# First products drained ahead of the slot's splits, and one difference of each pair a slot later

## The chip, the cores and the metric

The kernel runs on one core of one Trainium2 chip. The metric is the device time of one execution in microseconds; the time before is the median of three runs. A trace of one execution, taken by the hardware profiler, gives every instruction's start and length on the five engines: PE (TensorE, with PEld for its weight loads), DVE (VectorE), ACT (ScalarE), POOL (GpSimd) and SP (SyncE, which issues the transfers).

## The reference

```python
attn_out = _attn_ref(q, k, v, mem_k, mem_v)           # local attention, 4 x 8 x 768 x 64
x = attn_out.transpose(0, 2, 1, 3).reshape(3072, 512)
h = x @ w_in                                          # 512 -> 2048
x = (h * np.clip(h + 3.0, 0.0, 6.0) / 6.0) @ w_out    # 2048 -> 512
logits = x @ w_gate                                   # 8 experts
P = np.exp(logits - logits.max())
for _ in range(8):
    P /= P.sum(1, keepdims=True) + 1e-09
    P /= P.sum(0, keepdims=True) + 1e-09
    P *= N / E
for e in range(8):
    h = np.maximum(x @ w1[e], 0.0)                    # 512 -> 1024
    out += P[:, e:e + 1] * (h @ w2[e])                # 1024 -> 512
```

The change lies in the last loop, the eight experts.

## The kernel before, in words

All numbers are 32-bit. Every product is made of three matmuls: each operand is split into a rounded high part and the rest, and `passes` (lines 226 to 228) adds high x high, high x low and low x high in PSUM. ACT makes the high part, DVE the low part by subtracting.

The 3072 tokens are three blocks of 1024. One block with one expert is an n, so n runs from 0 to 23: block one is n = 0 to 7, block two 8 to 15, block three 16 to 23. In each n both expert products are done with seven products of half-size matrices in place of eight, so sums and differences of quarters of the operands stand around them.

- First products make h. `first_product` is a plain one: six matmuls of 512 columns into a bank ga or gc. `first_out` takes its result out of the bank (a drain): for k = 2 and p = 4 first ACT copies it (line 914), then DVE adds it into a tile g (line 920); p = 5 has only the add, p = 2 and 3 only a copy by ACT (line 916). In blocks two and three the last four of an n's first products (form `deep2`) are split further, with 256 columns; `deep_out` drains them (DVE line 903), and there several partial products follow one another in the same bank ga: the next matmul into ga needs the drain before it.
- `positive` makes a drained quarter non-negative on ACT (line 926), and POOL multiplies it by the gate's weights (line 933).
- Second products take h. `make(n, mi, part)` prepares the operand of product mi of n over four slots: part 0 splits its weights on ACT (line 843) and, where the operand is a difference of quarters of h, makes that on DVE for both halves (`g_sum`, line 959); parts 1 and 2 make the high halves on ACT (`oh`, line 979), parts 2 and 3 the low halves on DVE (`ol`, line 984). `second_out` adds a second product's result into y on DVE (line 1013).
- `w1_hi` (ACT line 806) and `w1_lo` (DVE line 811) split the weights of the first products. A low part is kept in DRAM and reloaded when the same weights come again, so that line 811 stands in block two only for weights that are new there, those of `deep2`, and in block three nowhere.

The order is written out by hand. The main loop goes through slots; a slot has one first product of n + 1 and one quarter of a second product of n on PE, and then issues, in this order on each engine: `second_out` of the slot before, `make`, the low parts of weights, a store, `positive` for the slot before, and last `first_out` of this slot's plain product and the next weights. Each engine works off its own queue in order.

Of the kernel before, what the change touches and what calls it, by code (L numbers as in the profile page):

```python
# [64 lines left out]
def attn_moe_moe(ctx: ExitStack, tc: tile.TileContext, qk, vw, wi, wo, wa, wb, wg, out):  # L65
# [4 lines left out]
    NE = wb.shape[0]  # L70
# [471 lines left out]
    def sinkhorn():  # L542
# [13 lines left out]
        for _ in range(8):  # L556
# [44 lines left out]
    SUMS = {"T1": ("B11", "B12", "B11"), "T2": ("T1", "B22", "T1"), "T3": ("B12", "B22", "B12"),  # L601
            "T4": ("T2", "B21", "T2")}
    X_ORDER = ("B21", "B11", "T1", "T2", "T3", "B22", "T4")
    NM = NSB * NE
# [224 lines left out]
    def w2_load(m):  # L829
        if m < 7 * NM:  # L830
            e, a = m // 7 % NE, SECOND[m % 7][0]
            s = w2s[m] = w2s_p.tile([128, 4, 256], F32, tag="w2s", name="w2s")
            if a >= S1:
                nc.sync.dma_start(out=s, in_=ws2[e][:, W2S[a]])
                return
            for g in range(2):
                of = wb[e, g].rearrange("p (c a d) -> p c a d", c=2, a=4)[:, :, {A11: 0, A12: 2, A22: 3}[a]]
                nc.sync.dma_start(out=s[:, 2 * g:2 * g + 2], in_=of)

    def w2_hi(m):  # L840
        if m < 7 * NM:
            hi = w2r_p.tile([128, 4, 256], F32R, tag="w2h", name="w2h", bufs=2)
            nc.scalar.activation(out=hi, in_=w2s[m], func=AF.Copy)  # L843
            w2[m] = hi
# [9 lines left out]
    def w2_lo_load(m):  # L854

        if 7 * NE <= m < 7 * NM:
            lo = w2l[m] = w2r_p.tile([128, 4, 256], F32R, tag="w2l", name="w2l", bufs=2)
            nc.sync.dma_start(out=lo.bitcast(F32), in_=wl2[m % (7 * NE)])

    def w2_lo_store(m):  # L860
        if m < 7 * NE:
            nc.sync.dma_start(out=wl2[m], in_=w2[m][1].bitcast(F32))
# [42 lines left out]
    def first_out(n, k, p):  # L905

        ps, b, i = ch[FIRST[p][2], k], FIRST_OUT[p], k // 2
        more = p == 4 and n >= NE
        for v in [b] * (p in (2, 3, 6)) + ["B21"] * more:
            if k % 2 == 0:  # L910
                gq[n, v, i] = g_p.tile([128, 2, HB], F32, tag="g", name="g", bufs=NG)
        g = gq[n, b, i][:, k % 2]
        if more:
            nc.scalar.activation(out=gq[n, "B21", i][:, k % 2], in_=ps, func=AF.Copy)  # L914
        if p in (2, 3):
            nc.scalar.activation(out=g, in_=ps, func=AF.Copy)
        elif p == 6:
            nc.scalar.activation(out=g, in_=ps, func=AF.Relu)
        else:
            nc.vector.tensor_tensor(out=g, in0=g, in1=ps, op=ALU.add)  # L920
# [33 lines left out]
    def g_sum(n, b, i):  # L954
        to, x, y = SUMS[b]
        o = gq[n, to, i]
        if n == NM - 1 and b == "T1":
            o = g_p.tile([128, 2, HB], F32, tag="g", name="g", bufs=NG)
        nc.vector.tensor_tensor(out=o, in0=gq[n, x, i], in1=gq[n, y, i], op=ALU.subtract)  # L959
        gq[n, b, i] = o  # L960

    def make(n, mi, part):

        m, b = 7 * n + mi, SECOND[mi][1]
        if part == 0:
            w2_hi(m)
            w2_lo_load(m)
            if b in SUMS and (n < NM - 1 or b in ("T2", "T4")):
                for i in range(2):
                    g_sum(n, b, i)  # L970
        if part == 1:
            w2_lo(m)
            w2_load(m + 1)
        if part == 3:
            w2_lo_store(m)
        if part in (1, 2):
            i = part - 1
            hi = op_p.tile([128, 2, HB], F32R, tag="oh", name="oh", bufs=3)
            nc.scalar.activation(out=hi, in_=gq[n, b, i], func=AF.Copy)  # L979
            op[m, i] = hi  # L980
        if part in (2, 3):
            i = part - 2
            lo = op_p.tile([128, 2, HB], F32R, tag="ol", name="ol", bufs=3)
            nc.vector.tensor_tensor(out=lo, in0=gq[n, b, i], in1=op[m, i].bitcast(F32), op=ALU.subtract)  # L984
            op[m, i] = op[m, i], lo
# [90 lines left out]
    with tc.manual_schedule():  # L1076
# [19 lines left out]
        for i, (pe, b, f) in enumerate(steps):  # L1096
# [74 lines left out]
            n = b + 1 if pe else 0  # L1171
# [49 lines left out]
        for n in range(NM):  # L1221
            for mi in range(7):
                for r in range(4):
                    i = at[n, mi - 1, r] if mi else at[n, 0, 0] - 4 + r
# [23 lines left out]
        for i, (h, o) in enumerate(order):  # L1248
            end = o and o[:2] == (NM - 1, 6)
            if h:  # L1250
                if h[1] in FORM:
                    for r in range(2):
                        deep_product(*h, r)
                        if o:
                            second_product(*o, (r,))
                else:
                    first_product(*h)
            if h and h[1] in FORM:
                pass
            elif end:  # L1260
                last_product(o[2])
            elif o:
                second_product(*o)
            if work and (i % 3 != 1 or i == 1) and next(work, 0) == 0:
                work = None
            if i in sums:
                x_sum(*sums[i])
            if before:
                second_out(*before)
            before = None if end else o  # L1270
            if end:
                last_out(o[2])
            if i in ends:
                g_sum(NM - 1, *ends[i])
            if h and h[1] in FORM:
                deep_out(*h, 0)
                while lows:
                    do, n = lows.pop(0)
                    do(n)
            for m in makes.get(i, ()):  # L1280
                make(*m)
            while lows:
                do, n = lows.pop(0)
                do(n)
            if i in gates_due:
                positive_gated(*gates_due.pop(i))
            for _ in range(2 if o and o[1] == 0 else 1):
                if left:
                    store(*left.pop(0))
            for w in after:  # L1290
                positive(*w)
            after = []
            if h and h[1] in FORM:
                n, _, p = h
                deep_out(*h, 1)
                if h[1] == DEEP2 and p > 1:
                    gates_due[i + (12 if n == NM - 1 and p == 3 else 1)] = n, p - 2
                if (h[1], p) == (DEEP, 2) and n >= 2:
                    gate_load(n)
                g = W1_AT[h]  # L1300
                if g:
                    lows.append((w1_lo, g + AHEAD - 1))
                    lows.append((w1_load, g + AHEAD + 3))
                else:
                    w1_load(AHEAD + 3)
                for m in range(AHEAD - 2 if g == 0 else 0):
                    w1_lo_store(m)
                w1_lo_store(g + AHEAD - 2)
            elif h:
                n, k, p = h  # L1310
                first_out(*h)
                if p in quarters:
                    after = [(n, k, quarters[p])]
                g = W1_AT[n, k // 2 * 2, p]
                if k % 2 == 0:
                    lows.append((w1_lo, g + AHEAD - 1))
                    w1_lo_store(g + AHEAD - 2)
            if h and (h[1] in FORM or h[1] % 2):
                if h[1] not in FORM:
                    w1_load(g + AHEAD + 3)  # L1320
                w1_lo_load(g + AHEAD)
                w1_hi(g + AHEAD)
            if i in fours:
                rows = []
                for q in range(2):
                    t = out_p.tile([128, HB], F32, tag="o", name="xs", bufs=NO)
                    nc.sync.dma_start(out=t, in_=x_source(*fours[i], q))
                    rows.append(t)
                quarter_work = i + 3, x_quarters(fours[i][1], *rows, nc.gpsimd)
            elif quarter_work and i >= quarter_work[0] and (i - quarter_work[0]) % 2 == 0:  # L1330
                if next(quarter_work[1], 0) == 0:
                    quarter_work = None
            for sb, r in halves.get(i, ()):
                x_half_load(sb, r + 2)
                if r >= 2:
                    x_half(r)
                    lows.append((x_half_low, r))
            if o and o[0] == NM - 1:
                for do, j in last.get(o[1:], ()):
                    do(j)  # L1340
            elif o and o[0] % NE == NE - 1 and o[1:] in ((5, 3), (6, 3)):
                left += [(o[0] // NE, j + 4 * (o[1] == 5)) for j in range(4)]
# [55 lines left out]
```

## Time and profile before

| | us |
|---|---|
| median of 3 runs (lowest, highest) | 2508.87 (2508.67, 2510.55) |
| profiled execution, its own time | 2509.96 |
| its span, from the first to the last instruction | 2508.2 |
| PE busy | 2491.2 |
| DVE busy | 1959.7 |
| ACT busy | 1444.9 |
| POOL busy | 910.8 |

The span is 1.8 us shorter than the execution's own time. PE's granted clock is 1.0 of full speed in every slice. The busy times overlap; what an engine does beside PE costs nothing as long as PE does not wait for it.

### The profile page before, as it was taken

The page shows a single profiled execution, that of the slowest core. Times are in us where ns is not written, and L with a number is a line of the kernel's source. Part 1 is how long each engine was busy: PE and PEld are TensorE (multiplying, and loading weights), DVE is VectorE, ACT ScalarE, POOL GpSimd, SP SyncE. Part 2 cuts the span into 40 slices and gives each one's busy share as a digit, 9 for nine tenths or more (in the row PEclk, how much of TensorE's full clock was granted, in tenths as well). Part 3 has the DMA queues.
Part 4 walks back from the last instruction along what each step waited for, and adds up shares of the span by engine and source line. Part 5 has one row for each costly group of instructions (what it writes and reads, how often), then busy time and mean ns, then how long its engine had stood idle before and what let it go on. Part 6 is the DMA issues. An engine that isn't in the chain of part 4 may idle for free. (4 is left out here: it accounts for less than half of the span.)

```text
span 2508.2 us, 37845 instructions
## 1 busy us (share of the span) xinstructions
PE 2491.2 (99%) x13525; PEld 2170.5 (87%) x13525; DVE 1959.7 (78%) x2432; ACT 1444.9 (58%) x2647; POOL 910.8 (36%) x705
## 2 busy tenths in 40 slices
PE   9999999999999999999999999999999999999999
PEld 8999999999878888888888888888888888888887
DVE  8866656576689999999986778777887677677677
ACT  8666652122365655556666655665566666555664
POOL 0155656564025544544442323232223322122320
PEclk9999999999999999999999999999999999999999
DMA  8689979877466666666777777666776677776664
GB/s 212 187 274 324 299 262 306 279 270 233 134 212 209 226 209 232 224 222 226 229 239 246 265 253 245 226 208 231 249 265 223 227 228 227 225 233 211 214 220 153
DMA packets 373753, 586.72 MB, mean 234 GB/s; under 512 B 30323, under 2 KB 227132, under 8 KB 373564
## 3 DMA queue, kind: packets, MB, share of 16 engines
q1 hardware_dynamic: 373280, 584.06, 71.5%
q8 instruction: 106, 1.74, 0.3%
q14 instruction: 83, 0.68, 0.1%
q10 hardware_dynamic: 284, 0.24, 0.0%
HBM read 443.57 MB, written 140.61 MB: 233 GB/s over the span
## 5 line engine op out<-in xcount | busy, mean ns | idle before, releaser
L933 POOL TENSOR_TENSOR g<-g,pb 128x512 f32<-128x512 f32 x304 | 533.2, 1766 | 1223.9 <-ACT g L926 818.6
L979 ACT ACTIVATE oh<-g 128x1024 fp32r<-128x1024 f32 x336 | 355.3, 1057 | 420.6 <-PE oa L228 200.5
L984 DVE TENSOR_TENSOR ol<-g,oh 128x1024 fp32r<-128x1024 f32 x336 | 470.9, 1402 | 91.7 <-ACT oh L979 91.5
L645 POOL TENSOR_TENSOR fr<-fr 128x256 f32<-128x256 f32 x320 | 270.7, 847 | 188.2 <-DMA fr<-in_wa_dram 100.5
L226 PE MATMUL ga<-xo,w1h 128*128 128x512 f32 (+1 forms) x864 | 314.8, 364 | 4.3 <-DVE g L903 3.4
L227 PE MATMUL ga<-xo,w1h 128*128 128x512 f32 (+1 forms) x864 | 312.2, 361 | 0.0
L228 PE MATMUL ga<-xo,w1l 128*128 128x512 f32 (+1 forms) x864 | 312.2, 361 | 0.0
L227 PE MATMUL oa<-ol,w2h 128*128 128x512 f32 x760 | 297.9, 392 | 1.5 <-DVE ol L984 1.4
L226 PE MATMUL oa<-oh,w2h 128*128 128x512 f32 x760 | 297.1, 391 | 0.0
L228 PE MATMUL oa<-oh,w2l 128*128 128x512 f32 x760 | 295.9, 389 | 0.0
L959 DVE TENSOR_TENSOR g<-g 128x1024 f32<-128x1024 f32 x192 | 290.6, 1553 | 0.0
L806 ACT ACTIVATE w1h<-w1s 128x512 fp32r<-128x512 f32 (+1 forms) x416 | 250.4, 602 | 47.6 <-issue 19.1
L926 ACT ACTIVATE g<-g 128x512 f32<-128x512 f32 x288 | 179.5, 623 | 124.0 <-DVE g L920 123.5
L920 DVE TENSOR_TENSOR g<-g,ga 128x512 f32<-128x512 f32 x192 | 130.5, 680 | 116.6 <-ACT g L914 113.4
L399 ACT ACTIVATE t<-ph,half 128x384 f32<-128x384 f32 x128 | 74.8, 584 | 241.4 <-PE ph L228 235.6
L226 PEld LDWEIGHTS ga<-xo,w1h 128*128 128x128 f32 x864 | 162.5, 188 | 40.3 <-DVE g L903 7.7
L843 ACT ACTIVATE w2h<-w2s 128x1024 fp32r<-128x1024 f32 x168 | 177.0, 1054 | 34.6 <-DMA w2s<-in_wb_dram 19.9
L226 PE MATMUL gc<-xo,w1h 128*128 128x512 f32 (+1 forms) x544 | 195.3, 359 | 1.0 <-ACT g L901 1.0
L228 PE MATMUL gc<-xo,w1l 128*128 128x512 f32 (+1 forms) x544 | 194.5, 357 | 0.0
L227 PE MATMUL gc<-xo,w1h 128*128 128x512 f32 (+1 forms) x544 | 194.3, 357 | 0.0
L227 PEld LDWEIGHTS ga<-xo,w1h 128*128 128x128 f32 x864 | 162.5, 188 | 28.3
L228 PEld LDWEIGHTS ga<-xo,w1l 128*128 128x128 f32 x864 | 162.4, 188 | 25.1
(184 smaller groups left out, 5774.7 us busy)
## 6 DMA issues: line engine op xcount, KB each, us to landing
w1l<-wl SPq DMA_DIRECT2D x232, 256.0 KB, 4.4
w2l<-wl SPq DMA_DIRECT2D x112, 512.0 KB, 3.7
w1s<-ws SPq DMA_DIRECT2D x192, 256.0 KB, 4.9
w2s<-ws SPq DMA_DIRECT2D x96, 512.0 KB, 5.6
ws<-fr SPq DMA_DIRECT2D x80, 512.0 KB, 5.1
w2s<-in_wb_dram SPq DMA_DIRECT2D x144, 256.0 KB, 4.3
wl<-w1l SPq DMA_DIRECT2D x128, 256.0 KB, 4.3
wl<-w2l SPq DMA_DIRECT2D x56, 512.0 KB, 4.9
```

Source lines behind the costliest of these rows:

```text
L226: nc.tensor.matmul(ps, wh, xh, start=start, stop=False, skip_group_check=more)
L227: nc.tensor.matmul(ps, wh, xl, start=False, stop=False, skip_group_check=more)
L228: nc.tensor.matmul(ps, wl, xh, start=False, stop=stop, skip_group_check=more)
L645: nc.gpsimd.tensor_tensor(out=o, in0=a, in1=b, op=f)
L806: nc.scalar.activation(out=w1_part(g, w1[g]), in_=w1_part(g, w1s[g]), func=AF.Copy)
L843: nc.scalar.activation(out=hi, in_=w2s[m], func=AF.Copy)
L920: nc.vector.tensor_tensor(out=g, in0=g, in1=ps, op=ALU.add)
L926: nc.scalar.activation(out=g, in_=g, func=AF.Relu)
L933: nc.gpsimd.tensor_tensor(out=g, in0=g, in1=p, op=ALU.mult)
L959: nc.vector.tensor_tensor(out=o, in0=gq[n, x, i], in1=gq[n, y, i], op=ALU.subtract)
L979: nc.scalar.activation(out=hi, in_=gq[n, b, i], func=AF.Copy)
L984: nc.vector.tensor_tensor(out=lo, in0=gq[n, b, i], in1=op[m, i].bitcast(F32), op=ALU.subtract)
```

## The change

For n from 8 on, `first_out` of a plain first product is issued before the slot's `make` calls and weights instead of after them. And from the second products of n = 7 on, the second of the two differences that `make` issues in part 0 (`g_sum` for half 1) goes to part 1, one slot later.

```diff
             if b in SUMS and (n < NM - 1 or b in ("T2", "T4")):
-                for i in range(2):
+                for i in range(1 if n >= NE - 1 else 2):
                     g_sum(n, b, i)
         if part == 1:
             w2_lo(m)
             w2_load(m + 1)
+            if b in SUMS and (NE - 1 <= n < NM - 1 or n == NM - 1 and b in ("T2", "T4")):
+                g_sum(n, b, 1)
...
                 while lows:
                     do, n = lows.pop(0)
                     do(n)
+            elif h and h[0] >= NE:
+                first_out(*h)
             for m in makes.get(i, ()):
                 make(*m)
             while lows:
...
                 n, k, p = h
-                first_out(*h)
+                if n < NE:
+                    first_out(*h)
                 if p in quarters:
                     after = [(n, k, quarters[p])]
```

No instruction is added or taken away. The queues of PE, POOL and SP have the same order as before; those of DVE and ACT change. Two places show it, both in the stretch in which the plain first products of n = 12 end and its `deep2` products begin, beside second products of n = 11.

DVE, before: ga is the bank of the plain products with p = 4 and then of `deep2`, gc that of p = 5; L984 is a low half ol, L959 a difference, L811 a low part of weights, L1013 an add into y.

```order
L984 TENSOR_TENSOR ol_16993<-g_16276,oh_16969 128x1024
L920 TENSOR_TENSOR g_16911<-g_16911,ga_16845 128x512
L1013 TENSOR_TENSOR y_14574<-y_14574,oa_16593 128x512
L959 TENSOR_TENSOR g_15787<-g_16045,g_15787 128x1024
L959 TENSOR_TENSOR g_15788<-g_16276,g_15788 128x1024
L811 TENSOR_TENSOR w1l_17019<-w1s_16838,w1h_16979 128x512
L920 TENSOR_TENSOR g_16911<-g_16911,ga_16866 128x512
L920 TENSOR_TENSOR g_16953<-g_16953,gc_16894 128x512
L1013 TENSOR_TENSOR y_14437<-y_14437,ob_17005 128x512
L984 TENSOR_TENSOR ol_17068<-g_15787,oh_17045 128x1024
L811 TENSOR_TENSOR w1l_17070<-w1s_16887,w1h_17028 128x512
L920 TENSOR_TENSOR g_16953<-g_16953,gc_16913 128x512
```

DVE, of the change, the same twelve instructions (lines after 972 are two higher, so that 984 is now 986 and 1013 now 1015):

```order
L920 TENSOR_TENSOR g_16907<-g_16907,ga_16844 128x512
L986 TENSOR_TENSOR ol_16996<-g_16274,oh_16970 128x1024
L1015 TENSOR_TENSOR y_14574<-y_14574,oa_16593 128x512
L920 TENSOR_TENSOR g_16907<-g_16907,ga_16866 128x512
L959 TENSOR_TENSOR g_15787<-g_16041,g_15787 128x1024
L811 TENSOR_TENSOR w1l_17020<-w1s_16837,w1h_16979 128x512
L920 TENSOR_TENSOR g_16948<-g_16948,gc_16894 128x512
L959 TENSOR_TENSOR g_15788<-g_16274,g_15788 128x1024
L1015 TENSOR_TENSOR y_14437<-y_14437,ob_17005 128x512
L920 TENSOR_TENSOR g_16948<-g_16948,gc_16913 128x512
L986 TENSOR_TENSOR ol_17069<-g_15787,oh_17046 128x1024
L811 TENSOR_TENSOR w1l_17071<-w1s_16887,w1h_17027 128x512
```

Each drain L920 has moved up by one to three places, and the second difference L959 has moved down past L811 and a drain. Behind both lists the same rows follow: the first `deep2` drain (L903 from ga), L984 or L986, the drain from gb, the add into y, the next L903 from ga.

ACT at the same place, before: L979 is a high half oh, L916 and L914 are copies out of a bank, L843 and L806 high parts of weights, L926 makes a quarter non-negative.

```order
L979 ACTIVATE oh_16969<-g_16276 128x1024
L916 ACTIVATE g_16953<-ga_16866 128x512
L806 ACTIVATE w1h_16979<-w1s_16838 128x512
L914 ACTIVATE g_16995<-ga_16845 128x512
L843 ACTIVATE w2h_17013<-w2s_16948 128x1024
L926 ACTIVATE g_16911<-g_16911 128x512
L914 ACTIVATE g_16995<-ga_16866 128x512
L806 ACTIVATE w1h_17028<-w1s_16887 128x512
L979 ACTIVATE oh_17045<-g_15787 128x1024
```

ACT, of the change:

```order
L916 ACTIVATE g_16948<-ga_16866 128x512
L981 ACTIVATE oh_16970<-g_16274 128x1024
L806 ACTIVATE w1h_16979<-w1s_16837 128x512
L914 ACTIVATE g_16993<-ga_16844 128x512
L914 ACTIVATE g_16993<-ga_16866 128x512
L843 ACTIVATE w2h_17015<-w2s_16950 128x1024
L926 ACTIVATE g_16907<-g_16907 128x512
L806 ACTIVATE w1h_17027<-w1s_16887 128x512
L981 ACTIVATE oh_17046<-g_15787 128x1024
```

The copy L914 of the second product now stands right behind that of the first, and the weights' L843 and the L926 that feeds POOL stand behind both.

## Rows read from the trace of the kernel before

**Rows 1.** The page, busy time, share of the span and instructions of each engine.

```profile
PE 2491.2 (99%) x13525; PEld 2170.5 (87%) x13525; DVE 1959.7 (78%) x2432; ACT 1444.9 (58%) x2647; POOL 910.8 (36%) x705
```

**Rows 2.** PE's waits from 1290 to 1860 us: total, times, longest.

```profile
PE ga L226 <- DVE g L903: 2.9, 7, 1.5
PE ga L226 <- ACT g L926: 0.8, 2, 0.5
```

**Rows 3.** Timeline of PE near 1610 us: start, length, instruction, idle time before.

```profile
1603.80 0.39 PE L226 MATMUL ob<-oh,w2h 128*128 128x512 f32 x1
...
1613.19 0.39 PE L228 MATMUL ob<-oh,w2l 128*128 128x512 f32 x1
1613.49 0.36 PE L226 MATMUL ga<-more,w1h 128*128 128x256 f32 x1
...
1616.75 0.39 PE L226 MATMUL ga<-xo,w1h 128*128 128x256 f32 x1 [0.21 <-DVE g L903]
```

**Rows 4.** Timeline of DVE in the same stretch.

```profile
1601.08 1.23 DVE L984 TENSOR_TENSOR ol<-g,oh 128x1024 fp32r<-128x1024 f32 x1 [1.45 <-ACT oh L979]
1602.57 0.69 DVE L920 TENSOR_TENSOR g<-g,ga 128x512 f32<-128x512 f32 x1 [0.26 <-ACT g L914]
...
1603.77 3.46 DVE L959 TENSOR_TENSOR g<-g 128x1024 f32<-128x1024 f32 x2
1607.15 0.68 DVE L811 TENSOR_TENSOR w1l<-w1s,w1h 128x512 fp32r<-128x512 f32 x1
...
1612.67 0.67 DVE L903 TENSOR_TENSOR g<-g,ga 128x512 f32<-128x512 f32 x1
1613.26 1.63 DVE L984 TENSOR_TENSOR ol<-g,oh 128x1024 fp32r<-128x1024 f32 x1
...
1616.02 0.67 DVE L903 TENSOR_TENSOR g<-g,ga 128x512 f32<-128x512 f32 x1
```

**Rows 5.** Timeline of ACT in the same stretch.

```profile
1599.98 1.06 ACT L979 ACTIVATE oh<-g 128x1024 fp32r<-128x1024 f32 x1 [3.54 <-PE oa L228]
...
1601.42 0.62 ACT L806 ACTIVATE w1h<-w1s 128x512 fp32r<-128x512 f32 x1
1601.95 0.59 ACT L914 ACTIVATE g<-ga 128x512 f32<-128x512 f32 x1
1602.42 1.06 ACT L843 ACTIVATE w2h<-w2s 128x1024 fp32r<-128x1024 f32 x1
1603.38 0.62 ACT L926 ACTIVATE g<-g 128x512 f32<-128x512 f32 x1
1604.00 0.60 ACT L914 ACTIVATE g<-ga 128x512 f32<-128x512 f32 x1
...
1610.86 1.06 ACT L979 ACTIVATE oh<-g 128x1024 fp32r<-128x1024 f32 x1 [1.77 <-PE ob L228]
```

**Rows 6.** Timeline of POOL in the same stretch.

```profile
1604.08 2.07 POOL L933 TENSOR_TENSOR g<-g,pb 128x512 f32<-128x512 f32 x1 [8.50 <-ACT g L926]
1609.17 1.29 POOL L933 TENSOR_TENSOR g<-g,pb 128x512 f32<-128x512 f32 x1 [3.03 <-ACT g L926]
1612.52 3.54 POOL L933 TENSOR_TENSOR g<-g,pb 128x512 f32<-128x512 f32 x2 [2.06 <-ACT g L926]
```

**Rows 7.** Timelines of POOL and DVE in block one, near 822 us.

```profile
820.80 2.27 POOL L933 TENSOR_TENSOR g<-g,pb 128x512 f32<-128x512 f32 x1
...
821.84 1.77 DVE L811 TENSOR_TENSOR w1l<-w1s,w1h 128x512 fp32r<-128x512 f32 x1
```

**Rows 8.** Timelines of PE and DVE at the same place of block three.

```profile
2150.11 0.28 PE L226 MATMUL ga<-more,w1h 128*128 128x256 f32 x1
...
2151.14 0.68 DVE L903 TENSOR_TENSOR g<-g,ga 128x512 f32<-128x512 f32 x1
...
2152.92 0.28 PE L226 MATMUL ga<-xo,w1h 128*128 128x256 f32 x1
```

**Rows 9.** Timeline of PE at the same place of n = 15.

```profile
1847.06 0.39 PE L226 MATMUL ga<-xo,w1h 128*128 128x256 f32 x1 [1.49 <-DVE g L903]
```

## The prediction

> **What bounds the kernel now.** I read the page first: PE is busy for 2491.2 of 2508.2 us [rows 1], so only its waits can be won, and whatever makes it wait longer is paid in full. Then PE's waits over block two: 2.9 us for DVE's drain L903 and 0.8 us put down to ACT's L926 [rows 2]. The timelines show where both lie: at one place of each n, where its `deep2` products begin. There the matmuls into ga come in three groups, and each needs the drain of the one before.
>
> From the second group (1613.49) to the third (1616.75) it takes 3.26 us [rows 3], in block three from 2150.11 to 2152.92, 2.81 [rows 8]. So a place costs 0.45 us now. DVE is what is late: behind 1602.57 no row of its shows idle time before it, its queue has been full since, and the two L903 come at 1612.67 and 1616.02 [rows 4]. There are eight places, n = 8 to 15; those of n = 9 to 14 are alike, n = 15 has a longer wait, 1.49 us [rows 9]. In block three, where L811 is gone, the second L903 ends 1.10 us before PE needs it (2151.14 + 0.68 against 2152.92) [rows 8].
>
> **The change part by part.** The same instructions run, the transfers keep their order, and the matmuls too. So the question is whether DVE reaches the two L903 sooner or later. Durations for that:
> - A 512-wide DVE instruction hands over after 0.60 (1612.67 to 1613.26), a 1024-wide one of 1.23, with the same overlap of 0.08, after 1.14 [rows 4].
> - On ACT 0.47 to 0.53 after a 512-wide one, 0.96 after a 1024-wide one (1602.42 to 1603.38) [rows 5]. L926 takes 0.62, and POOL's multiply starts 0.08 behind it (1604.00, 1604.08) [rows 5, 6].
> - A copy L914 starts 0.20 after PE's group is over (1603.80, 1604.00) [rows 3, 5].
> - DVE and POOL shut each other out. A multiply alone takes 1.29; that of 1604.08 took 2.07, so it stood until 1604.86, when the first difference (from 1603.77) had run 1.09; then the second difference stood until the multiply ended at 1606.15, and DVE's next instruction began 1.00 later, at 1607.15 [rows 4, 6]. L811 can be shut out too: 1.77 against 0.68, with its end 0.54 after the multiply's [rows 7]. A drain out of PSUM is not: L903 at 1612.67 took 0.67 under a multiply [rows 4, 6]. Who asks first, runs first.
>
> Now the queues of the change at this place. ACT: L916 has gone ahead, so behind L979 (1599.98) come L806 at 1600.94 and the first L914 at 1601.47, 0.48 sooner than now. But the drain that waits for it now heads DVE's queue, ahead of the L984 that could run at 1601.08. So DVE starts at 1602.08 in place of 1601.08: the drain, L984 at 1602.68, L1013 at 1603.82, free at 1604.42. The second L914 cannot start before 1604.00, since PE is not done sooner; it ends at 1604.60, the drain starts at 1604.62, the first difference at 1605.22 (now 1603.77, with that drain still to come: 0.85 us net late).
>
> ACT's L843 and L926 now stand behind that second L914: 1604.47 and 1605.43 to 1606.05. The first multiply asks at 1606.13; the first difference lets go at 1605.22 + 1.09 = 1606.31. By 0.18 the multiply is first. It runs to 1607.60, and L811, next on DVE, hands over at 1608.06 in place of 1606.96. Then the drain from gc, and at 1608.66 the second difference. Meanwhile ACT has done L806, L979 (1606.48) and L926 (1607.44 to 1608.06), so the second multiply runs under the drain from 1608.14 to 1609.43, and the difference hands over at 1610.43. L1013, the drain of the last plain product at 1611.03, L984 from 1611.63, letting go at 1612.72. The third multiply asks at 1612.52, as now, since the L979 ahead of it waits for PE until 1610.86 both times. It is first by 0.20, runs to 1614.01, and L811 hands over at 1614.47. So the first L903 starts at 1614.47 against 1612.67, and PE, 0.15 after its end, at 1615.29 against 1613.49. The fourth multiply follows when L811 lets go (about 1614.5 to 1615.8) and holds the next L984, which hands over at 1616.8; then the drain of gb and L1013; the second L903 at 1618.0 against 1616.02. PE goes on at 1618.73 in place of 1616.75: **2.0 us lost per place**.
>
> The six like places make 12.0. Those of n = 8 and n = 15 have the same steps and one or two more splits in DVE's queue (0.60 to 1.14 each), in which a multiply can fall; for these I take 2.5 each, 5.0. Block three: without L811 DVE has 1.1 us to spare behind the last drain [rows 8] and the 0.85 of lateness fits into it, so 0. The differences that move elsewhere (a slot later, at three other products of each n) end in L984; PE waits for none in this stretch [rows 2], and ACT's oh of the second half stands waiting for PE there (1599.98 after 3.54 us, 1610.86 after 1.77) [rows 5], so 0 again; if that cover went, a late L979 would first delay the L914 behind it on ACT, then the drains. Sum 17.0: 2509.96 + 17.0 = 2527.0 for an execution like the profiled one, whose time is 1.1 us above the median; on the median 2508.87 + 17.0 = **2525.9**.
>
> Bounds per place. Below: if the shut-outs disappear, DVE's late start is made up and PE's loss goes, a gain of 0.45. Above: one more full shut-out, 1.29 less the 0.6 it would find covered, 2.7 in all. I stand near the upper end because two of the three orders are settled by 0.18 and 0.20 us, and the handovers above repeat within 0.06.
>
> **The rivals.**
> - *The third multiply comes second.* If DVE is 0.2 us sooner at 1612.5, L811 goes first (free at 1613.3 in place of 1614.47), only the next L984 is held, and the second L903 comes 0.5 to 0.6 late. Eight places: 2513.3. For it: 0.20 is small. Against: that instant hangs on the end of the second multiply, which hangs on ACT alone.
> - *No change.* If the first multiply asks 0.18 later, L811 goes first, the second difference is held by the first multiply alone, DVE reaches the first L903 at 1612.2, and the second, held by the third multiply as now, at 1616.0. The loss stays at 0.45 a place: 2509.
> - *Faster.* The drains do not need what POOL holds, so that multiplies that fall under L920 and L903 cost DVE nothing. If all four fall so, DVE reaches the second L903 by 1615.2 instead of 1616.02, and PE's losses go: six times 0.45, and for n = 8 and 15 what the waits hold beside the six short ones of 0.21, 3.7 less 1.3 [rows 2, 3]; 5.1 in all, 2503.8. It decides when the first and the third multiply ask 0.2 us later than worked out. [...]
>
> **How the numbers follow.** The measurement can tell about 0.2%, 5.0 us: 2503.9 to 2513.9. Forecast 0.60 (2519 to 2531, its own range, 1.3 to 2.7 a place), third multiply second 0.14 (2511 to 2517, half of it beyond 2513.9), no change 0.16 (2506 to 2512), faster 0.10 (2501 to 2506, six in ten below 2503.9). That makes slower 0.60 + 0.07 = 0.67, faster 0.06, same 0.27. The range goes down from 2531 until two in ten are left out: to 2508.
>
> **What would show it.** Right: PE's waits for L903 between 1290 and 1860 grow from 2.9 us to 15 or more, none appear in block three; at each place of n = 9 to 14 L811 lasts 1.8 us; DVE idles about 2.5 us before the drain that waits for L914 (now 1.45 + 0.26). Wrong: L811 at 0.68 with PE's waits unchanged or gone; or waits at a new name, L984 before a second product, which would mean that the difference moved by a slot is what is late.

## The result and the profile after

The changed kernel takes 2529.98 us (median of 6 runs, 2527.95 to 2533.16) against 2508.77 for the kernel before in the same comparison (6 runs, 2508.49 to 2510.55): 1.0085 times as long, 95% interval 1.0072 to 1.0098, so 21.2 us slower. The forecast was 2525.9, slower, with a range of 2508 to 2531. Place, mechanism and sign came out as worked; 4.1 us are missing in the sum.

The page of the profiled execution (2533.16 us, its span 2531.4), which answers to [rows 1]:

```profile
PE 2501.7 (99%) x13525; PEld 2181.1 (86%) x13525; DVE 1946.1 (77%) x2432; ACT 1445.8 (57%) x2647; POOL 922.6 (36%) x705
```

The span has grown by 23.2 us. PE is busy 10.5 us longer with the same 13525 matmuls, and idle 12.7 us longer (29.7 against 17.0). The idle time is of the kind that was forecast, though less of it than the 17.0 of the sum. The longer busy time was not in the sum.

PE's waits from 1290 to 1880 us, against [rows 2] (total, times, longest); in block three, 1880 to 2470, PE waits for no engine:

```profile
PE ga L226 <- DVE g L903: 17.1, 11, 2.9
```

Now the place of n = 12 that the prediction worked through, against [rows 3 to 6]. It comes 13.37 us later than before (ACT's L981, the former L979, at 1613.35 against 1599.98), so 13.37 is to be taken from each start. DVE's timeline:

```profile
1615.45 0.69 DVE L920 TENSOR_TENSOR g<-g,ga 128x512 f32<-128x512 f32 x1 [2.39 <-ACT g L914]
...
1618.06 0.69 DVE L920 TENSOR_TENSOR g<-g,ga 128x512 f32<-128x512 f32 x1 [0.19 <-ACT g L914]
1618.67 1.22 DVE L959 TENSOR_TENSOR g<-g 128x1024 f32<-128x1024 f32 x1
1619.80 1.78 DVE L811 TENSOR_TENSOR w1l<-w1s,w1h 128x512 fp32r<-128x512 f32 x1
1621.51 0.68 DVE L920 TENSOR_TENSOR g<-g,gc 128x512 f32<-128x512 f32 x1
1622.11 1.90 DVE L959 TENSOR_TENSOR g<-g 128x1024 f32<-128x1024 f32 x1
...
1625.12 1.21 DVE L986 TENSOR_TENSOR ol<-g,oh 128x1024 fp32r<-128x1024 f32 x1
1626.26 1.77 DVE L811 TENSOR_TENSOR w1l<-w1s,w1h 128x512 fp32r<-128x512 f32 x1
1627.95 0.67 DVE L903 TENSOR_TENSOR g<-g,ga 128x512 f32<-128x512 f32 x1
1628.55 1.69 DVE L986 TENSOR_TENSOR ol<-g,oh 128x1024 fp32r<-128x1024 f32 x1
...
1631.36 0.68 DVE L903 TENSOR_TENSOR g<-g,ga 128x512 f32<-128x512 f32 x1
```

ACT's timeline at the same place:

```profile
1614.84 0.58 ACT L914 ACTIVATE g<-ga 128x512 f32<-128x512 f32 x1
1617.43 0.60 ACT L914 ACTIVATE g<-ga 128x512 f32<-128x512 f32 x1 [2.01 <-PE ga L228]
1617.93 1.05 ACT L843 ACTIVATE w2h<-w2s 128x1024 fp32r<-128x1024 f32 x1
1618.88 0.62 ACT L926 ACTIVATE g<-g 128x512 f32<-128x512 f32 x1
```

POOL's timeline:

```profile
1619.57 1.47 POOL L933 TENSOR_TENSOR g<-g,pb 128x512 f32<-128x512 f32 x1 [10.98 <-ACT g L926]
1621.64 1.29 POOL L933 TENSOR_TENSOR g<-g,pb 128x512 f32<-128x512 f32 x1 [0.60 <-DVE w1l L811]
1625.94 3.21 POOL L933 TENSOR_TENSOR g<-g,pb 128x512 f32<-128x512 f32 x2 [3.01 <-ACT g L926]
```

And PE's, the two groups of `deep2` into ga, and between them two matmuls of 512 columns:

```profile
1628.77 0.36 PE L226 MATMUL ga<-more,w1h 128*128 128x256 f32 x1 [1.76 <-DVE g L903]
...
1629.56 0.40 PE L226 MATMUL oa<-oh,w2h 128*128 128x512 f32 x1
1629.79 0.40 PE L227 MATMUL oa<-ol,w2h 128*128 128x512 f32 x1
...
1632.09 0.39 PE L226 MATMUL ga<-xo,w1h 128*128 128x256 f32 x1 [0.26 <-DVE g L903]
```

Read them as a chain. DVE stands 2.39 us for ACT's copy, where before it stood 1.45 for a high half of ACT's and 0.26 for the copy [rows 4]. ACT stands 2.01 for PE before the second copy, and only then come L843 and the L926 that lets POOL start. POOL's multiply asks at 1619.57, while the difference of 1618.67 runs; when that lets go the multiply goes first, and L811 behind it lasts 1.78 in place of 0.68. The third multiply (1625.94) does the same to the next L811. So both L903 are late, and PE stands 1.76 and 0.26 us.

What the prediction did not have stands behind some of these waits. PE's timeline at the place of n = 8:

```profile
1308.53 0.55 PE L226 MATMUL ga<-more,w1h 128*128 128x256 f32 x1 [2.88 <-DVE g L903]
1308.88 0.41 PE L227 MATMUL ga<-more,w1h 128*128 128x256 f32 x1
...
1309.94 0.63 PE L226 MATMUL oa<-oh,w2h 128*128 128x512 f32 x1
1310.37 0.63 PE L227 MATMUL oa<-ol,w2h 128*128 128x512 f32 x1
```

A matmul of 512 columns follows the last after 0.43 us (1309.94 to 1310.37), where at n = 12 it is 0.23 (1629.56 to 1629.79). The windows give the granted clock; after the time come PE, PEld, DVE, ACT and POOL, then the clock:

```profile
1300.00:1305.00 5.00, 5.00 (x29) 4.38 (x28) 5.00 (x7) 1.30 (x3) 1.29 (x1) 1.00 0.33 100
1309.00:1313.00 4.00, 4.00 (x17) 3.61 (x16) 3.38 (x6) 0.00 (x0) 0.00 (x0) 0.50 0.87 289
1471.00:1474.00 3.00, 3.00 (x16) 2.71 (x15) 3.00 (x5) 0.01 (x1) 0.11 (x1) 0.61 0.77 212
1629.00:1632.00 3.00, 2.82 (x18) 2.22 (x17) 3.00 (x5) 0.90 (x2) 0.15 (x1) 1.00 0.73 220
```

Before PE's wait at n = 8 the clock is 1.00 of full speed; behind it 0.50. The third window is behind the wait of n = 10 and mixes the two levels, the fourth is n = 12 and stays at the upper one. In this execution the lower level follows the waits of n = 8, 10, 11, 13 and 15 (0.50 in a window of 2 us behind each), and not those of n = 9, 12 and 14 (1.00 in the 3 us behind each).

What the lower level adds at a like place shows from the first group of one n to that of the next. PE, at n = 11 and n = 13:

```profile
1549.76 0.36 PE L226 MATMUL ga<-more,w1h 128*128 128x256 f32 x1 [1.77 <-DVE g L903]
...
1706.82 0.36 PE L226 MATMUL ga<-more,w1h 128*128 128x256 f32 x1 [1.78 <-DVE g L903]
```

From n = 11 to n = 12 it takes 79.01 us, with the lower level behind the wait of n = 11, and from n = 12 to n = 13 78.05, without it. Before, it took 76.10 from the third group of n = 11 to that of n = 12 (1616.75, [rows 3]):

```profile
1540.65 0.39 PE L226 MATMUL ga<-xo,w1h 128*128 128x256 f32 x1 [0.20 <-DVE g L903]
```

So a like place costs about 1.9 us, and 2.9 with the lower level.

### The profile page after: what moved, and what is told of

The parts are those of the page before. It is cut to its first block, busy times and chain, and to the rows that moved or that the text cites. A ratio compares the mean times of both kernels' runs of the same rounds, so it can differ in the third digit from the quotient of the medians.

```text
span 2531.4 us, 37810 instructions
## 1 busy us (share of the span) xinstructions
PE 2501.7 (99%) x13525; PEld 2181.1 (86%) x13525; DVE 1946.1 (77%) x2432; ACT 1445.8 (57%) x2647; POOL 922.6 (36%) x705
## 4 chain that ended last, share of the span: by engine, by line
PE 92%; DVE 5%; issue 1%; DMA 1%; ACT 1%; SPq 0%; DVEq 0%; ACTq 0%
PE ga L226 7%; PE ga L228 7%; PE ga L227 7%; PE oa L227 7%; PE oa L226 7%; PE oa L228 7%; PE gc L226 4%; PE gc L227 4%; PE gc L228 4%; PE pa L226 4%; PE ph L226 4%; PE pa L228 3%; PE pa L227 3%; PE ph L228 3%; PE ph L227 3%; PE oc L227 3%
## 5 line engine op out<-in xcount | busy, mean ns | idle before, releaser
L933 POOL TENSOR_TENSOR g<-g,pb 128x512 f32<-128x512 f32 x304 | 545.3, 1809 | 1236.9 <-ACT g L926 754.4
L981 ACT ACTIVATE oh<-g 128x1024 fp32r<-128x1024 f32 x336 | 355.4, 1058 | 370.1 <-PE oa L228 124.1
L986 DVE TENSOR_TENSOR ol<-g,oh 128x1024 fp32r<-128x1024 f32 x336 | 461.1, 1374 | 52.4 <-ACT oh L981 52.2
L806 ACT ACTIVATE w1h<-w1s 128x512 fp32r<-128x512 f32 (+1 forms) x416 | 250.0, 601 | 67.3 <-issue 29.4
L959 DVE TENSOR_TENSOR g<-g 128x1024 f32<-128x1024 f32 x192 | 269.9, 1425 | 0.0
L920 DVE TENSOR_TENSOR g<-g,ga 128x512 f32<-128x512 f32 x192 | 131.5, 685 | 158.0 <-ACT g L914 126.4
L926 ACT ACTIVATE g<-g 128x512 f32<-128x512 f32 x288 | 178.1, 619 | 52.2 <-DVE g L920 52.0
L843 ACT ACTIVATE w2h<-w2s 128x1024 fp32r<-128x1024 f32 x168 | 177.0, 1053 | 34.2 <-DMA w2s<-in_wb_dram 22.3
```

The lines of the kernel that those rows point to most:

```text
L806: nc.scalar.activation(out=w1_part(g, w1[g]), in_=w1_part(g, w1s[g]), func=AF.Copy)
L926: nc.scalar.activation(out=g, in_=g, func=AF.Relu)
L933: nc.gpsimd.tensor_tensor(out=g, in0=g, in1=p, op=ALU.mult)
```

## The experiments

Three theories stood against each other: the drains of p = 4, put ahead, start DVE late, and POOL's multiplies turn that into long waits (the prediction's); the moved difference is what is late; and, for the part that was missing, the lower clock behind the waits.

**The drains alone.** The change without its two edits to `g_sum`:

```diff
-                for i in range(1 if n >= NE - 1 else 2):
+                for i in range(2):
                     g_sum(n, b, i)
...
-            if b in SUMS and (NE - 1 <= n < NM - 1 or n == NM - 1 and b in ("T2", "T4")):
-                g_sum(n, b, 1)
```

Expected: 

> Only the first part of the change: the plain drains stand ahead, both differences of a pair stay together. My theory (a drain at the head of DVE's queue waits for ACT's L914, and POOL's multiplies then hold the splits L811 and L984): the first drain L903 of each deep2 place starts about 2 us later than before, 1.8 to 2.4, and the time is 2526 to 2532 us. Rival (the difference that moved by a slot is what makes DVE late): this kernel is where before is, 2507 to 2511 us.

Measured: 2532.16 us (2530.11 to 2532.74), 1.0087 times as long as before (1.0074 to 1.0101), 0.2 us above the range that was expected. PE's waits in block two:

```profile
PE ga L226 <- DVE g L903: 21.7, 13, 3.7
```

Two windows of the same run, behind the waits of n = 9 and n = 12:

```profile
1392.00:1396.00 4.00, 3.69 (x15) 3.42 (x16) 3.91 (x6) 1.06 (x1) 0.70 (x1) 0.57 0.85 260
...
1629.00:1633.00 4.00, 3.73 (x25) 3.07 (x24) 3.86 (x7) 2.55 (x3) 0.00 (x0) 1.00 0.90 249
```

The whole loss is there without the moved difference. The first waits of n = 9 to 14 are longer, 2.15 to 2.16 us, yet among these six only the one of n = 9 has the lower clock behind it (0.57 in that window, 1.00 in like ones behind the other five).

**The difference alone.** The change without its edits to the slot loop:

```diff
-            elif h and h[0] >= NE:
-                first_out(*h)
...
-                if n < NE:
-                    first_out(*h)
+                first_out(*h)
```

Expected: 

> Only the second part: the second difference goes to the next slot, all drains stay behind the slot's splits and weights. My theory: the difference lets two drains pass; the first L903 of a place starts about 0.8 us sooner than before, at which the wait for the second is decided by 0.02 us between the third multiply and the low half L984: 2504 to 2509 us. Rival (the moved difference is the cause): 2520 us or more.

Measured: 2510.67 us (2508.34 to 2512.32, 11 runs), ratio 1.0004 (0.9995 to 1.0013). PE's waits in block two:

```profile
PE ga L226 <- ACT g L926: 5.0, 2, 2.5
```

So the moved difference costs nothing measurable as a whole, and that rival falls. But the time is 1.7 us above the range that was expected. At the six like places PE's wait is gone; the two that are left, 2.47 and 2.51 us, lie at n = 8 and n = 15, and behind the second the clock falls (0.96 over 1840 to 1880).

**The p = 4 drains back behind.** The whole change, but for this:

```diff
-            elif h and h[0] >= NE:
+            elif h and h[0] >= NE and h[2] != 4:
                 first_out(*h)
...
-                if n < NE:
+                if n < NE or p == 4:
                     first_out(*h)
```

Expected: 

> The change with one exception: the drains of p = 4, which wait for ACT's copy L914, stay where they were, behind make and the weights; those of p = 2, 3 and 5 stand ahead. My theory: no DVE instruction waits for L914 with L984 ready behind it, so the late start of 0.85 us goes and with it the shut-out of L811 by the third multiply; L903 starts 0.9 us sooner than before, PE's wait at the places of n = 9 to 14 goes: 2503 to 2508 us. Rival (the drains in general, or the weights pushed behind them on ACT, are the cause): half or more of the loss stays, 2519 us or more.

Measured: 2510.94 us (2508.95 to 2514.04, 11 runs), ratio 1.0005 (0.9996 to 1.0014). Waits in block two:

```profile
PE ga L226 <- DVE g L903: 5.1, 2, 3.0
```

Some 19 of the 21.2 us are gone: the drains of p = 4 cause them. What else went ahead, the add of p = 5 and the copies of p = 2 and 3, changes nothing beside the difference alone. Again it is 3 us above what was expected, by the waits at n = 8 (3.0) and n = 15 (2.1).

**No multiplies in block two.** Line 933 is left out for n = 8 to 15, so that the gate's weights don't enter there:

```diff
-        nc.gpsimd.tensor_tensor(out=g, in0=g, in1=p, op=ALU.mult)
+        if n // NE != 1:
+            nc.gpsimd.tensor_tensor(out=g, in0=g, in1=p, op=ALU.mult)
```

Expected: 

> The changed kernel without POOL's multiplies L933 in block two (n = 8 to 15): the gate's weights are left out there, so the output is not the reference's. My theory (1.1 us of the 2 lost per place come from multiplies that hold L811, the difference and L984, and without any the late start of 0.85 is made up): PE's waits for L903 in block two fall from 17.1 us to under 3, 2503 to 2509 us. Rival (the drain's wait for ACT alone is the cause): some 1 us per place stays, 2515 us or more.

Measured, in one run: 2504.6 us. DVE's timeline at n = 12 (960 and 987 are the change's 959 and 986):

```profile
1600.16 0.69 DVE L920 TENSOR_TENSOR g<-g,ga 128x512 f32<-128x512 f32 x1 [2.39 <-ACT g L914]
...
1604.51 0.69 DVE L811 TENSOR_TENSOR w1l<-w1s,w1h 128x512 fp32r<-128x512 f32 x1
...
1609.32 0.69 DVE L811 TENSOR_TENSOR w1l<-w1s,w1h 128x512 fp32r<-128x512 f32 x1
1609.93 0.68 DVE L903 TENSOR_TENSOR g<-g,ga 128x512 f32<-128x512 f32 x1
```

PE's waits in block two:

```profile
PE ga L226 <- DVE g L903: 0.4, 1, 0.4
```

DVE still stands 2.39 us for ACT's copy, but L811 is back at 0.69 both times, and PE waits 0.4 us in all of block two. The late start alone is harmless; it costs because POOL's multiplies then shut out the splits. In the change L811, begun at 1619.80 behind the multiply of 1619.57, takes 1.78, and here without the multiplies 0.69.

**The add ahead of the copy.** In the whole change, ACT's copy out of the bank (line 914) is issued behind DVE's add:

```diff
-        if more:
-            nc.scalar.activation(out=gq[n, "B21", i][:, k % 2], in_=ps, func=AF.Copy)
...
             nc.vector.tensor_tensor(out=g, in0=g, in1=ps, op=ALU.add)
+        if more:
+            nc.scalar.activation(out=gq[n, "B21", i][:, k % 2], in_=ps, func=AF.Copy)
```

Expected: 

> The changed kernel with one pair turned round: for p = 4 DVE's add L920 comes ahead of ACT's copy L914 out of the same bank, so that DVE waits for PE alone and ACT waits for DVE. Theory (the drain's wait for L914 at the head of DVE's queue starts the lateness): DVE starts its two p = 4 drains 0.6 to 0.8 us sooner, the first multiply comes after the first difference has let go and the first split L811 is through, the first L903 of a place starts at or ahead of where it did in the kernel before: 2505 to 2513 us. Rival (what matters is that the weights' L843 and the L926 that feeds POOL stand behind both copies on ACT, whoever waits for whom): 2522 us or more.

Measured: 2514.55 us (2511.41 to 2519.28, 10 runs), ratio 1.0022 (1.0013 to 1.0031). DVE's timeline at n = 12, where line 918 is the add:

```profile
1604.99 0.69 DVE L918 TENSOR_TENSOR g<-g,ga 128x512 f32<-128x512 f32 x1 [1.66 <-PE ga L228]
...
1609.45 0.69 DVE L811 TENSOR_TENSOR w1l<-w1s,w1h 128x512 fp32r<-128x512 f32 x1
...
1615.20 0.68 DVE L811 TENSOR_TENSOR w1l<-w1s,w1h 128x512 fp32r<-128x512 f32 x1
```

PE's waits in block two:

```profile
PE ga L226 <- DVE g L903: 7.6, 8, 3.3
```

Without the wait for the copy L811 escapes: POOL's first multiply starts at 1610.57, when it is through. 15.4 us of the loss go, with the drains still ahead and the difference still moved. Of the 7.6 us that are left n = 8 has 3.34 and n = 15 some 2; the six like places have about 0.37 each. The result is 1.6 us above the range that was expected. Behind both ends the clock falls (0.89 over 1290 to 1320, 0.96 over 1840 to 1880).

**The wait filled.** In the change, PE does eight more matmuls of 512 columns, by zeroed weights and so without effect, into the bank ob ahead of the `deep2` group that waits, at each of the eight places:

```diff
+                    if h[1:] == (DEEP2, 0) and h[0] // NE == 1:
+                        nn, mi, q = o
+                        for _ in range(FILL):
+                            nc.tensor.matmul(yo[SECOND[mi][2], q // 2], ones.bitcast(F32R), op[7 * nn + mi, 1][0][:, 1],
+                                             start=False, stop=True, skip_group_check=True)
...
+            if i == at[4, 0, 0]:
+                nc.vector.tensor_scalar_mul(ones.bitcast(F32R), ident, 0.0)
```

Expected: 

> The changed kernel, with eight more matmuls of 512 columns with zero weights (they add zero into ob) at each of the eight places, just where PE waits for the first drain L903; no drain moves by it. Theory: the slow matmuls behind the wait (0.43 us instead of 0.23 for 512 columns) come from PE standing idle for 1.8 us and more: with the wait filled (8 x 0.23 = 1.8 us) they go, the six like places end where they did, and the time is 2522 to 2526 us, some 5 below the changed kernel. Rival (PE is slow there whatever it does ahead, for instance because its weights or operands come late): slow matmuls stay, 2528 us or more.

Measured: 2526.46 us (2525.12 to 2530.17), ratio 1.0070 (1.0054 to 1.0085), 3.5 us below the change itself, with 64 matmuls more. The windows that had 0.50 and 0.61:

```profile
1309.00:1313.00 4.00, 4.00 (x28) 3.58 (x27) 3.86 (x7) 0.99 (x2) 0.00 (x0) 1.00 1.01 332
1471.00:1474.00 3.00, 2.72 (x18) 2.46 (x18) 2.15 (x5) 1.22 (x2) 0.00 (x0) 1.00 0.99 337
```

PE's waits in block two (its lines are one higher here):

```profile
PE ga L227 <- DVE g L904: 4.6, 9, 1.0
```

The drain is still late, but PE stands idle for it for 1.0 us at most, and the clock stays at its upper level, 1.00 in both windows: its mean over the whole execution is 1.000, where the change had 0.995. So it is the idle stretch that lowers the clock here, and not late weights or operands. By the medians this costs about 3.5 us, a rough figure, since the two intervals overlap. Between the two profiled executions it is 6.4 us (spans of 2531.4 and 2525.0), but the change's is the slowest of its six. The filling adds next to nothing of its own at n = 12: from the start of the last matmul ahead of it to that of the first group it takes 2.18 us (1621.97 to 1624.15), in the change with the wait 2.15 (1626.62 to 1628.77). What stays is the loss without the clock: 17.7 us by the medians and 16.8 by the spans, where the prediction had 17.0. The median is 0.5 us above the range that was expected.

**The difference where it helped.** The kernel before, with only the second difference a slot later, and only for second products of n = 8 to 13, away from both ends:

```diff
-                for i in range(2):
+                for i in range(1 if NE <= n < 2 * NE - 2 else 2):
                     g_sum(n, b, i)
...
+            if b in SUMS and NE <= n < 2 * NE - 2:
+                g_sum(n, b, 1)
```

Expected: 

> The kernel before, with the second difference one slot later only for the second products of n = 8 to 13, which stand beside the six like deep2 places (n = 9 to 14); n = 8 and 15 keep their order. My theory (there the pair of differences in one piece is what keeps DVE late; at n = 8 and 15, where more splits stand in DVE's queue, the moved difference costs more than it saves): PE's wait goes at the six places, 0.6 us each with the slower first matmuls, and nothing is added at the two others: 2504 to 2506 us against 2509 of before. Rival (the gain at the six places in the run with the difference alone hung on the shifted timing of n = 8): 2508 to 2510 us.

Measured: 2505.58 us (2504.55 to 2508.52, 11 runs) against 2509.51 before, ratio 0.9985 (0.9977 to 0.9994): 3.9 us faster, and faster than both kernels. DVE's timeline at n = 12:

```profile
1600.37 1.22 DVE L959 TENSOR_TENSOR g<-g 128x1024 f32<-128x1024 f32 x1
1601.50 1.79 DVE L811 TENSOR_TENSOR w1l<-w1s,w1h 128x512 fp32r<-128x512 f32 x1
...
1603.81 1.21 DVE L959 TENSOR_TENSOR g<-g 128x1024 f32<-128x1024 f32 x1
...
1607.28 0.68 DVE L811 TENSOR_TENSOR w1l<-w1s,w1h 128x512 fp32r<-128x512 f32 x1
...
1608.48 0.68 DVE L903 TENSOR_TENSOR g<-g,ga 128x512 f32<-128x512 f32 x1
```

PE's waits in block two:

```profile
PE ga L226 <- DVE g L903: 1.5, 1, 1.5
PE ga L226 <- ACT g L926: 0.8, 2, 0.5
```

L811 is shut out once, the pair of differences no longer is (1.22 and 1.21 against 3.46 for the two in [rows 4]). DVE is in time, and only the waits of the two ends are left. From the first group of n = 8 (1304.07) to the third of n = 15 (1841.71) PE takes 3.76 us less than before (1305.66 to 1847.06), some 0.6 at each of the six places, where the prediction put the old price of a place at 0.45.

## Why the prediction was right, and where it was short

**The late start: right.** With 13.37 taken off, the first drain starts at 1602.08 (worked out: 1602.08), the second at 1604.69 (1604.62), the first difference at 1605.30 (1605.22). The add ahead of the copy shows that it is the wait for the copy that starts the chain.

**Who comes first on DVE and POOL: right.** The first multiply asks at 1606.20 (1606.13), the third at 1612.57 (1612.52). Both went first, though the margins on paper were only 0.18 and 0.20 us, and they did so at all six like places: each L811 of 512 columns there lasts 1.77 or 1.78, and the first waits are 1.76 to 1.78. With this all three rivals fall, each of which had one of the two come second.

**The price of a like place: right.** The first L903 starts at 1614.58 (1614.47), PE goes on at 1615.40 (1615.29) and, for the third group, at 1618.72 (1618.73). Against 1616.75 [rows 3] that is 1.97 us lost, where 2.0 was in the sum.

**The ends: about right in sum, but not as worked.** The first waits are 2.88 us at n = 8 and 2.80 at n = 15, against 0.28 and 0.51 for ACT's L926 there before. The 1.49 of [rows 9] is gone, by the author's estimate in part because PE, at the lower clock, comes later to it: from the first group to the third it takes 5.26 us there (1864.94 to 1870.20), against 3.05 before (1842.52 to 1847.06, less the 1.49). The prediction put the differences that move elsewhere at 0 and set the ends apart by splits alone. That does not hold: on its own the moved difference makes waits of 2.5 us at each end, while it wins at the six like places, and the two cancel (2510.67). Beside the drains that stand ahead it helps: with the drains alone the first waits of the ends are 3.72, and those of the like places 2.15 to 2.16. Why the ends differ from the like places was not tried by a run; that more splits stand in DVE's queue there was only argued.

**Block three: right.** No wait appears there.

**The term that was short: PE's pace after a wait.** The step that failed is the plain sum, 17.0 us as waits alone. It took PE to go on at its old pace. Counted from start to start of the slow matmuls, against 0.23 us for 512 columns and 0.12 for 256 at the upper level, the lower one cost 9.7 us in the profiled execution: 2.7 behind the wait of n = 8, 2.6 behind that of n = 15, and 1.4 to 1.5 each at n = 10, 11 and 13. The other 13.5 of the 23.2 us are the waits' part. That is less than 17.0, in part because a slower PE comes later to the next drain: the 0.26 that PE stands at n = 12 for its third group is missing at n = 10, 11 and 13. So for this execution the prediction's 2527.0 was too high in the waits and had nothing for the clock, and 2533.16 came out. The other executions had less of the lower level or as much: the mean clock was 0.995 in the two slowest (2532.61 and 2533.16) and 0.997 or 0.998 in the other four (2527.95 to 2530.61). That the median stayed within the range is in part luck, since nothing in the range had allowed for the clock.

**Open.** Which wait is followed by the lower clock, and why it differs from execution to execution, no run here shows. Length alone doesn't decide it: of the change's six like waits of 1.77 three had it (n = 10, 11, 13), of the six of 2.16 with the drains alone one did. With the p = 4 drains behind, the 3.0 at n = 8 had not (clock 1.00 over 1290 to 1320), and the 2.1 at n = 15 had (0.96 over 1840 to 1880).

## What to carry to other kernels

A drain put ahead in a queue brings its own wait to the head of that queue (here 2.39 us for ACT's copy): ask first whom it waits for, and what on other engines stands behind the same release. Where DVE and POOL shut each other out, work out for each POOL instruction what DVE runs when it asks, since the order can hang on a few tenths of a microsecond: here the first multiply came some 0.2 us before the difference let go, and L811 paid 1.1 us. And when PE is made to wait inside a dense stretch, allow for its pace after the wait too, as a range, since not every wait is followed by the lower clock (three of six of 1.77 us here).

## What the runs showed of the hardware

Behind waits of 1.77 us the granted clock fell from 1.00 to 0.50 at three of six like places (n = 10, 11 and 13); a matmul of 512 columns then took 0.43 us in place of 0.23, and the place cost 2.9 us in place of 1.9. Matmuls by zeroed weights, in place of the wait, kept the clock at its upper level (a mean of 1.000 over the profiled execution, 0.995 without them). A DVE subtraction of 128x512 with both operands in SBUF took 0.69 us alone and 1.78 where a POOL multiply was ahead of it, and a drain out of PSUM took 0.68 under a multiply (1621.51, the multiply at 1621.64).
